# Decoding attention with a gated feed-forward on one core: inputs packed in order of use, all products on TensorE

## The chip, the cores and the metric

The kernel runs on one core of a Trainium2 chip. The metric is device microseconds of one execution, as the median of several runs. A core has TensorE (PE; its weight loads are PEld), VectorE (DVE), ScalarE (ACT), GpSimd (POOL) and SyncE (SP, which here only issues transfers), an on-chip memory of 128 partitions (SBUF), accumulators for TensorE (PSUM), and 16 DMA engines that move data between the chip's memory and SBUF. Everything is float32.

## The reference

One token goes through an attention block over a cached context of 8192 positions, then through a gated feed-forward block, each behind a layer norm and with a residual:

```python
B, Sq, D = 1, 1, 640
H, Sk, Dh = 32, 8192, 192        # k_cache, v_cache: (1, 32, 8192, 192)
...
q = (layernorm(x) @ wq) split into 32 heads of 192
scores = einsum("bhqd,bhkd->bhqk", q, k_cache) * (Dh ** -0.5)
o = einsum("bhqk,bhkd->bhqd", softmax(scores), v_cache)
h = x + o @ wo                    # wq (640, 6144), wo (6144, 640)
...
gate, up = layernorm(h) @ W_gate, layernorm(h) @ W_up      # (640, 1536)
h2 = h + (relu(gate) * up) @ W_down                        # (1536, 640)
```

K and V are 201 MB each, and all weights together 43 MB. Every byte is read once and used for one product, so the work is a stream of 446 MB.

## The kernel before

The work goes head by head, in the program order of one Python loop; a tile framework puts in the waits.

**Transfers.** SP issues all loads in program order. `load_kv` (L77 to L84) brings K or V of one head as one transfer of 128 partitions with 49,152 bytes each into one of three buffers `kv_t`; a load is issued when the tile that had this buffer has been used up. `load_wo` (L86 to L92) brings the rows of `wo` for four heads (two at the end). `wq` comes first, in three transfers through the same buffers. The last loads are W_up, W_gate in two parts and W_down in six (L359 to L363). In all SP issues 89 loads of 128 partitions each: 32 of K, 36 for V (the last head's in five), 9 of `wo`, 3 of `wq`, and 9 for the feed-forward; each partition's piece is a packet on one of the 16 DMA engines, so each engine moves 8 packets per load.

**Scores.** In `head_step` (L181 to L194) DVE multiplies K with the query in four pieces (L188), POOL adds the upper half of each product to the lower (L189), and DVE sums what is left (L193).

**Softmax** (`softmax_steps`, L196 to L215): maximum over partitions through a TensorE transpose (L200), exponential on ACT (L206), the sum over partitions on TensorE (L208).

**Values.** In `values_of` (L234 to L256) TensorE takes 40 of the 64 positions of a partition, as 20 products of two positions with 384 columns (`pairs`, L226 to L231), ACT scales 12 (L240) and DVE 12 (L241), and POOL adds these up (L246). The last two heads' values go to TensorE entirely (`values_last`).

**After a head** `finish_steps` (L289 to L321) sums over partitions on TensorE (L299), transposes on DVE (L303) and multiplies with `wo` (L276, L319). At the end come the layer norm (L368 to L387), the two projections (L392) and the product with W_down (L409), which starts on each part of W_down as it lands, and one output transfer (L413).

A matmul in float32 shows as two records of PE, each with its weight load; four matmuls on the four groups of 32 columns of the array run side by side, and four such records are called a set below.

Of the kernel before, what the change touches and what calls it, by code (L numbers as in the profile page):

```python
# [1 line left out]

# [8 lines left out]
AX = mybir.AxisListType  # L11


@with_exitstack
def kernel(
    ctx: ExitStack,
    tc: tile.TileContext,
    x: bass.AP,
    kc: bass.AP,
    vc: bass.AP,  # L20
    wq: bass.AP,
    wo: bass.AP,
    w_gate: bass.AP,
    w_up: bass.AP,
    w_down: bass.AP,
    out: bass.AP,
):
# [48 lines left out]

    def load_kv(src, h, parts):  # L77
        t = kv.tile([P, 2 * TW], F32, name="kv_t")
        v = src[h].rearrange("(p r) d -> p (r d)", p=P)
        b = 0  # L80
        for n in parts:
            nc.sync.dma_start(t[:, b:b + n], v[:, b:b + n])  # L82
            b += n
        return t  # L84

    def load_wo(gi):  # L86
        hs = GROUPS[gi]
        j = len(hs) * DH // P
        t = wts.tile([P, j, D], F32, tag="wo_t", name="wo_t")
        r0 = hs[0] * DH  # L90
        nc.sync.dma_start(t, wo[r0:r0 + len(hs) * DH, :].rearrange("(p j) n -> p j n", p=P))
        return t  # L92

    ones = const.tile([P, P], F32, name="ones")
    nc.gpsimd.memset(ones, 1.0)
    eps = const.tile([P, 1], F32, name="eps")
    nc.gpsimd.memset(eps, EPS)
    ident = const.tile([P, P], F32, name="ident")
    from concourse.masks import make_identity
    make_identity(nc, ident)  # L100

    sel = const.tile([P, NQ, P], F32, name="sel")
    nc.gpsimd.memset(sel, 0.0)
    for g in range(NQ):
        nc.gpsimd.memset(sel[g * Q:g * Q + 1, g, :], 1.0)

    par = const.tile([P, 2, Q], F32, name="par")
    for i in range(2):
        nc.vector.reduce_sum(par[:, i, 0:1], ident.rearrange("p (g c) -> p g c", c=Q)[:, :, i], axis=AX.X)
        nc.vector.tensor_copy(par[:, i, 1:Q], par[:, i, 0:1].to_broadcast([P, Q - 1]))  # L110

    def rstd_of(dst, var, name):

        ve = const.tile([P, 1], F32, name=f"ve{name}")
        nc.vector.tensor_scalar_add(ve, var, EPS)
        sd = const.tile([P, 1], F32, name=f"sd{name}")
        nc.scalar.activation(sd, var, AF.Sqrt, bias=eps)
        y = const.tile([P, 1], F32, name=f"y{name}")
        nc.vector.reciprocal(y, sd)
        t = const.tile([P, 1], F32, name=f"t{name}")  # L120
        nc.vector.scalar_tensor_tensor(t, y, ve, y, op0=ALU.mult, op1=ALU.mult)
        nc.vector.tensor_scalar(t, t, -0.5, 1.5, op0=ALU.mult, op1=ALU.add)
        nc.vector.tensor_mul(dst, y, t)


    s1 = const.tile([P, 1], F32, name="s1")
    nc.vector.reduce_sum(s1, xT, axis=AX.X)  # L127
    pm = ps_s.tile([P, 512], F32, name="ps_small")
    nc.tensor.matmul(pm[:, 0:1], ones, s1, start=True, stop=True)
    mean = const.tile([P, 1], F32, name="mean")  # L130
    nc.vector.tensor_scalar_mul(mean, pm[:, 0:1], 1.0 / D)
    xc = const.tile([P, DJ], F32, name="xc")
    nc.vector.tensor_scalar(xc, xT, mean, None, op0=ALU.subtract)
    xsq = const.tile([P, DJ], F32, name="xsq")
    nc.vector.tensor_mul(xsq, xc, xc)
    s2 = const.tile([P, 1], F32, name="s2")
    nc.vector.reduce_sum(s2, xsq, axis=AX.X)
    pv = ps_s.tile([P, 512], F32, name="ps_small")
    nc.tensor.matmul(pv[:, 0:1], ones, s2, start=True, stop=True)
    var = const.tile([P, 1], F32, name="var")  # L140
    nc.vector.tensor_scalar_mul(var, pv[:, 0:1], 1.0 / D)
    rstd = const.tile([P, 1], F32, name="rstd")
    rstd_of(rstd, var, "x")
    xn = const.tile([P, DJ], F32, name="xn")
    nc.vector.tensor_scalar_mul(xn, xc, rstd)


    acc = ps_a.tile([P, DG], F32, name="acc")
    for g in range(NQ):
        nc.tensor.matmul(acc[g * Q:(g + 1) * Q, :], ones[0:1, 0:Q], xrow[:, g * DG:(g + 1) * DG],  # L150
                         start=True, stop=False)


    qps = [ps_q.tile([P, QB], F32, tag="q", name=f"qp{b}") for b in range(2)]
    qps.append(ps_x.tile([P, QB], F32, tag="x", name="qp2"))
    for j in range(DJ):
        for b in range(NQB):
            for g in range(NQ):
                c0 = g * HPQ * DH + b * QB
                nc.tensor.matmul(qps[b][g * Q:(g + 1) * Q, :], xn[:, j:j + 1].to_broadcast([P, Q]),  # L160
                                 wq_ts[j][:, c0:c0 + QB], start=(j == 0), stop=(j == DJ - 1))
    q4 = const.tile([P, HPQ * DH], F32, name="q4")
    for b in range(NQB):
        nc.scalar.mul(q4[:, b * QB:(b + 1) * QB], qps[b], SCALE)  # L164

    pair_of = {}

    def query(h):

        g, i = divmod(h, HPQ)  # L170
        if i % 2 == 0:
            q = ps_q.tile([P, QB], F32, tag="q", name="q")
            nc.tensor.matmul(q[:, 0:2 * DH], sel[:, g, :], q4[:, i * DH:(i + 2) * DH], start=True, stop=True)  # L173
            pair_of[h // 2] = q
        return pair_of[h // 2][:, (i % 2) * DH:(i % 2 + 1) * DH]

    HD = DH // 2

    keep = tc.keep_in_program_order

    def head_step(q, kt, *works):  # L181


        sc = small.tile([P, NS], F32, name="sc")
        k3 = kt.rearrange("p (r d) -> p r d", d=DH)
        parts = [(i0, k3[:, i0:i0 + SUB, :]) for i0 in range(0, NS, SUB)]
        for i0, ks in parts:
            keep(nc.vector.tensor_mul(ks, ks, q[:, None, :].to_broadcast([P, SUB, DH])))  # L188
            nc.gpsimd.tensor_add(ks[:, :, 0:HD], ks[:, :, 0:HD], ks[:, :, HD:DH])  # L189
            for w in works:  # L190
                next(w, None)
        for i0, i1 in ((0, NS // 2), (NS // 2, NS - SUB), (NS - SUB, NS)):
            keep(nc.vector.reduce_sum(sc[:, i0:i1], k3[:, i0:i1, 0:HD], axis=AX.X))  # L193
        return sc  # L194

    def softmax_steps(sc, res):  # L196
# [15 lines left out]
        keep(nc.vector.reciprocal(rl, pl[:, 0:1]))  # L212
        nc.scalar.mul(pn, p, rl)  # L213
        res += [pn]
        yield  # L215

# [123 lines left out]
    for _ in done:  # L342
        pass
# [97 lines left out]
```

## Time and profile before

| what | before |
|---|---|
| median of 3 runs | 1044.37 us (1044.22 to 1044.38) |
| profiled execution, from first to last instruction | 1042.8 us |
| DVE, POOL busy | 779.6 us (75%), 776.5 us (74%) |
| PE, ACT busy | 311.4 us (30%), 161.8 us (16%) |
| loads: share of the 16 DMA engines' span | 99.3% |
| moved | 446.28 MB, 428 GB/s |

The profile has no time of its own for the profiled execution beside its span of 1042.8 us; the median of the runs is 1.6 us above this span. That is what lies around the span: the runs count from before the first recorded instruction to after the last. Sums below are made against the span, and 1.6 us is added at the end. Shares are of the span; "idle before" in a group of instructions is the time that its engine stood still just ahead of it, with the releaser behind the arrow.

### The profile page before, as it was taken

What the parts mean: (1) busy time and instruction counts of PE and PEld (TensorE: products, weight loads), DVE (VectorE), ACT (ScalarE), POOL (GpSimd) and SP (SyncE); (2) the same over time, 40 slices, a digit from 0 to 9 for tenths busy, and PEclk for the clock granted to TensorE, in tenths of its full rate; (3) what the DMA queues carried; (4) which work ended last, traced back from release to release, by engine and by line L of the source; (5) the groups of instructions that cost most, each with busy time, mean ns of one, the idle gap of its engine ahead of it and who ended that gap; (6) DMA issues with size and microseconds to landing.
All of it is one profiled execution on the core that took longest, in us unless ns stands there. A gap on an engine that the chain in (4) does not pass through costs nothing.

```text
span 1042.8 us, 5875 instructions
## 1 busy us (share of the span) xinstructions
PE 311.4 (30%) x2056; PEld 91.5 (9%) x2056; DVE 779.6 (75%) x445; ACT 161.8 (16%) x471; POOL 776.5 (74%) x321
## 2 busy tenths in 40 slices
PE   1603232222234212232322222242222323230376
PEld 0100000000000000000000000000000000010122
DVE  1087988688888888688986888788886889878641
ACT  0101111011111101111110111111111111110110
POOL 0057888788887888688897888868886888888730
PEclk9955655665656556566666656565565665565577
DMA  9999999999999999999999999999999999999997
GB/s 392 446 430 432 425 441 426 437 427 436 432 434 430 428 438 424 439 425 440 432 432 430 434 432 430 433 432 434 430 423 441 436 432 430 432 436 424 433 423 307
DMA packets 12998, 446.28 MB, mean 428 GB/s; under 512 B 1573, under 2 KB 1577, under 8 KB 3114
## 3 DMA queue, kind: packets, MB, share of 16 engines
q1 hardware_dynamic: 12824, 445.92, 99.3%
q8 instruction: 16, 0.26, 0.1%
q14 instruction: 12, 0.10, 0.0%
q10 hardware_dynamic: 146, 0.01, 0.0%
HBM read 445.91 MB, written 0.00 MB: 428 GB/s over the span
## 4 chain that ended last, share of the span: by engine, by line
DMA 77%; DVE 14%; PE 5%; POOL 3%; issue 1%; ACT 0%; SPq 0%; ACTq 0%; POOLq 0%; DVEq 0%
DMA kv_t<-in_A_k_cache_dram 70%; DVE kv_t L188 12%; DMA ffn_b<-in_B_W_down_dram 3%; PE ps_small L299 2%; DMA kv_t<-in_A_v_cache_dram 2%; DMA xrow<-in_A_x_dram 2%; POOL kv_t L246 2%; PE ps_small L200 1%; POOL kv_t L189 1%; DVE sc L193 1%; PE qp L160 1%; DVE kv_t L241 1%; DVE mp L198 0%; PE pd L409 0%; SPq L82 0%
## 5 line engine op out<-in xcount | busy, mean ns | idle before, releaser
L188 DVE TENSOR_TENSOR kv_t<-kv_t,q 128x3072 f32<-128x3072 f32 x128 | 427.4, 3342 | 182.8 <-DMA kv_t<-in_A_k_cache_dram 182.4
L189 POOL TENSOR_TENSOR kv_t<-kv_t 128x1536 f32<-128x1536 f32 x128 | 438.2, 3448 | 96.1 <-DVE kv_t L188 85.1
L246 POOL TENSOR_TENSOR kv_t<-kv_t 128x1152 f32<-128x1152 f32 (+1 forms) x180 | 337.2, 1874 | 125.7 <-DVE kv_t L241 80.7
L193 DVE TENSOR_REDUCE sc<-kv_t 128x16 f32<-128x1536 f32 (+1 forms) x96 | 213.2, 2273 | 0.7 <-POOL kv_t L189 0.7
L230 PE MATMUL po<-kv_t,pn 128*2 128x384 f32 x1328 | 162.0, 653 | 104.1 <-DMA kv_t<-in_A_v_cache_dram 104.1
L200 PE MATMUL ps_small<-ident,mp 128*128 128x128 f32 x32 | 14.2, 444 | 449.0 <-DVE mp L198 449.0
L240 ACT ACTIVATE kv_t<-kv_t,pn 128x192 f32<-128x192 f32 x360 | 127.8, 441 | 101.9 <-DMA kv_t<-in_A_v_cache_dram 98.4
L241 DVE TENSOR_TENSOR kv_t<-kv_t,pn 128x2304 f32<-128x2304 f32 x30 | 103.3, 3444 | 0.0
L206 ACT ACTIVATE p<-sc,m 128x64 f32<-128x64 f32 x32 | 11.1, 348 | 583.7 <-DVE m L203 583.7
L230 PEld LDWEIGHTS po<-kv_t,pn 128*2 128x2 f32 x1328 | 38.1, 103 | 219.1 <-issue 219.1
L200 PEld LDWEIGHTS ps_small<-ident,mp 128*128 128x128 f32 x32 | 5.8, 180 | 471.7 <-issue 426.9
L276 PE MATMUL acc<-wo_t,oT 128*3 128x480 f32 x112 | 32.8, 898 | 18.0 <-DVE oT L303 18.0
L173 PE MATMUL q<-q,sel 128*128 128x384 f32 x32 | 20.7, 747 | 56.9 <-DVE kv_t L188 56.9
L208 PE MATMUL ps_small<-rs,ones 128*128 128x1 f32 x64 | 18.6, 359 | 59.7 <-ACT p L206 59.7
L213 ACT ACTIVATE pn<-p,rl 128x64 f32<-128x64 f32 x32 | 11.1, 348 | 102.7 <-DVE rl L212 102.7
L299 PE MATMUL ps_small<-kv_t,ones 128*32 128x192 f32 (+1 forms) x64 | 24.8, 508 | 2.2 <-POOL kv_t L246 2.2
L208 PEld LDWEIGHTS ps_small<-rs,ones 128*128 128x128 f32 x64 | 15.8, 307 | 86.2 <-ACT p L206 74.5
L303 DVE STREAM_TRANSPOSE oT<-ps_small 32x192 f32<-32x192 f32 (+1 forms) x32 | 11.7, 364 | 10.2 <-PE ps_small L299 9.5
L160 PE MATMUL qp<-kv_t,xn 128*32 128x512 f32 x120 | 17.2, 737 | 5.5 <-DMA kv_t<-in_A_wq_dram 3.1
L242 DVE TENSOR_TENSOR kv_t<-po,par 128x384 f32<-128x384 f32 x30 | 16.3, 544 | 0.0
L268 DVE MEMSET acc<- 128x512 f32 x1 | 0.5, 485 | 20.9 <-ACT q L164 20.9
L127 DVE TENSOR_REDUCE s<-xT 128x1 f32<-128x5 f32 x1 | 0.2, 157 | 17.1 <-DMA xT<-in_A_x_dram 17.1
(82 smaller groups left out, 102.7 us busy)
## 6 DMA issues: line engine op xcount, KB each, us to landing
kv_t<-in_A_k_cache_dram SPq DMA_DIRECT2D x32, 6144.0 KB, 24.1
kv_t<-in_A_v_cache_dram SPq DMA_DIRECT2D x31, 6144.0 KB, 23.2
wo_t<-in_A_wo_dram SPq DMA_DIRECT2D x7, 1920.0 KB, 27.1
kv_t<-in_A_wq_dram SPq DMA_DIRECT2D x2, 6144.0 KB, 17.8
ffn_a<-in_B_W_up_dram SPq DMA_DIRECT2D x1, 3840.0 KB
kv_t<-in_A_wq_dram SPq DMA_DIRECT2D x1, 3072.0 KB, 40.0
kv_t<-in_A_v_cache_dram SPq DMA_DIRECT2D x1, 3072.0 KB, 17.2
kv_t<-in_A_v_cache_dram SPq DMA_DIRECT2D x4, 768.0 KB, 20.8
```

What stands on the lines that cost most here:

```text
L160: nc.tensor.matmul(qps[b][g * Q:(g + 1) * Q, :], xn[:, j:j + 1].to_broadcast([P, Q]), wq_ts[j][:, c0:c0 + QB], start=(j == 0), stop=(j == ...
L188: keep(nc.vector.tensor_mul(ks, ks, q[:, None, :].to_broadcast([P, SUB, DH])))
L189: nc.gpsimd.tensor_add(ks[:, :, 0:HD], ks[:, :, 0:HD], ks[:, :, HD:DH])
L193: keep(nc.vector.reduce_sum(sc[:, i0:i1], k3[:, i0:i1, 0:HD], axis=AX.X))
L200: keep(nc.tensor.transpose(pt[:, 0:P], mp.to_broadcast([P, P]), ident))
L208: nc.tensor.matmul(pl[:, 0:1], ones, rs, start=True, stop=True)
L230: nc.tensor.matmul(po[g * Q:g * Q + 2, :], pn[:, 2 * i:2 * i + 2], vt[:, 2 * i * DH:(2 * i + 2) * DH], start=(i < NQ), stop=(i >= n - NQ))
L240: nc.scalar.activation(v3[:, r, :], v3[:, r, :], AF.Copy, scale=pn[:, r:r + 1])
L241: keep(nc.vector.tensor_mul(v3[:, RV:NS, :], v3[:, RV:NS, :], pn[:, RV:NS, None].to_broadcast([P, RN, DH])))
L246: nc.gpsimd.tensor_add(v3[:, r:r + n, :], v3[:, r:r + n, :], v3[:, s:s + n, :])
L276: nc.tensor.matmul(acc3[g * Q:g * Q + 3, 0:W3], oT[:, t:t + 3, 0], w3[:, g * W3:(g + 1) * W3], start=(gi == 0 and t == 0), stop=(gi == LAS ...
L299: nc.tensor.matmul(pt[q0:q0 + Q, 0:W], par[:, k, :] if n > 1 else ones[:, 0:Q], ob[:, k * DH + u * W:k * DH + (u + 1) * W], start=(k == 0) ...
```

## The change

The kernel is written anew, without the tile framework.

- **Packing.** On the host (`pack`) the inputs are laid out in the order of use, 128 partitions wide. A turn of three heads is five rows: four of 65,280 bytes a partition and one of 56,832. K comes transposed (the 192 elements of a position across partitions), the columns of `wq` for a head and the rows of `wo` for a head lie beside it. A first row of 57,088 bytes holds head 0's K, the first query weights and x; four tail rows hold the last heads, and W_up, W_gate and W_down follow, W_down in four pieces. That makes 61 loads of 128 partitions.
- **Buffers.** Three slots X, Y, Z of 65,280 bytes a partition. Row 1 goes to X, 2 to Z, 3 to Y, 4 to X, 5 to Y. A slot is loaded again when semaphores say that all of it has been used.
- **Products.** TensorE computes queries (from a DVE product, L392 to L394), scores (24 matmuls of 512 columns a head, `pe_k`), values (32 of 384 columns a head, `pe_v`) and the head's output (`pe_o`). DVE transposes scores, takes maxima and adds the `wo` product; ACT copies and takes the exponential; POOL only fills constants.
- **Loops.** Each engine has its own program; ten turns run as a hardware loop on PE, DVE, ACT and SP.

```diff
-        for i0, ks in parts:
-            keep(nc.vector.tensor_mul(ks, ks, q[:, None, :].to_broadcast([P, SUB, DH])))
-            nc.gpsimd.tensor_add(ks[:, :, 0:HD], ks[:, :, 0:HD], ks[:, :, HD:DH])
...
-            kt = load_kv(kf, h + 1, [2 * TW])
-            vt = load_kv(vf, h, [2 * TW])
...
+DOWN = ((0, 6 * D), (6 * D, 10 * D), (10 * D, 11 * D + D // 2), (11 * D + D // 2, 12 * D))
...
+        rows[0][i] = cat(kw[a], qw(b), va[:, :8 * PW])
+        rows[1][i] = cat(va[:, 8 * PW:], ow(a - 1), kw[b][:, :12 * 512])
+        rows[2][i] = cat(kw[b][:, 12 * 512:], qw(c), vb[:, :24 * PW])
+        rows[3][i] = cat(vb[:, 24 * PW:], ow(b - 1), kw[c])
+        rows[4][i] = cat(qw(c + 1), vv, ow(c - 1))
...
+    def pe_k(blk, before=(None, None)):
+        for half in range(2):
+            if before[half] is not None:
+                wait(te, before[half], 16)
+            for part in range(3):
+                for g in range(4):
+                    m = te.matmul(sc[Q(g), half * 512:half * 512 + 512], qs[:, 32 * part:32 * part + 32],
+                                  blk(half, part * 4 + g), start=(part == 0), stop=(part == 2))
+            op(m, inc=p2d)
...
+            m = te.matmul(po[32 * g:32 * g + 2, 0:PW], p[:, 2 * i:2 * i + 2], blk(i), start=(i < 4), stop=(i >= 28))
...
+        with te.Fori(0, NTURN):
+            wait(te, land[1], 16)
+            pe_unit(ka, (None, None), va, (land[2], None), free[1], inc_at=(7, free[1]))
+            pe_unit(kb, (None, land[3]), vb, (None, land[4]), free[3], inc_at=(23, free[3]))
+            pe_unit2()
...
+    def dve_unit(wo_t, w_next, relay=None, q_wait=None):
+        dve_scores()
+        if relay is not None:
+            wait(ve, ds, cnt.n).then_inc(relay, 1)
...
+            dve_unit(woa, wqb)
+            dve_unit(wob, wqc, relay=free[2])
+            wait_row5 = (land[5], 16)
+            dve_unit(woc, wqa, relay=free[4], q_wait=wait_row5)
+            settle()
+            ve.sem_inc(free[5], 1)
...
+        def turn(i):
+            load(Y[:, 0:W_3], r3[i], land[3])
+            wait(sp, free[1], 2, 2)
+            wait(sp, land[1], 16, 16)
+            load(X[:, 0:W_4], r4[i], land[4])
+            wait(sp, free[2], 1, 1)
+            wait(sp, land[2], 16, 16)
+            wait(sp, free[3], 2, 2)
+            wait(sp, land[3], 16, 16)
+            load(Y[:, 0:W_5], r5[i], land[5])
+            wait(sp, free[4], 1, 1)
+            wait(sp, land[4], 16, 16)
+
+        with sp.Fori(0, NTURN - 1) as i:
+            turn(i)
+            load(X[:, 0:W_1], r1[i + 1], land[1])
+            load(Z[:, 0:W_2], r2[i + 1], land[2])
+            wait(sp, free[5], 1, 1)
+            wait(sp, land[5], 16, 16)
...
+        for n, (a, b) in enumerate(DOWN):
+            load(X[:, W_UP + a:W_UP + b], dram["row_down"][:, a:b], tl[f"d{n}"])
```

SP's loads in the steady stage before, one head and a half (names in brackets are the framework's semaphores of the engines and of earlier loads):

```order
L82 DMA kv_t<-in_A_k_cache_dram 128x12288 [waits DVE_49,DMAHW2_49,PE_49,Activation_49]
L82 DMA kv_t<-in_A_v_cache_dram 128x12288 [waits DMAHW6_49,DMAHW3_49,DVE_49]
L91 DMA wo_t<-in_A_wo_dram 128x3840
L82 DMA kv_t<-in_A_k_cache_dram 128x12288 [waits DVE_49,DMAHW4_49,PE_49,Activation_49]
L82 DMA kv_t<-in_A_v_cache_dram 128x12288 [waits DMAHW5_49,DVE_49]
```

SP's loop of one turn now (`land` counts a row that has landed, `free` says that a slot is used up):

```order
L544 DMA slot_y<-row 128x16320
L544 DMA slot_x<-row 128x16320 [waits free1,land1]
L544 ISA [waits free2,land2,free3,land3]
L544 DMA slot_y<-row 128x14208
L544 ISA [waits free4,land4]
L544 DMA slot_x<-row 128x16320
L544 DMA slot_z<-row 128x16320
L567 REGISTER_ALU [waits free5,land5]
L567 COMPARE_AND_BRANCH
```

Six transfers of K and V and three quarters of one of `wo` have become five; each load still stands behind waits for its slot. The load of the next turn's row 1 into X waits for `free4`, which DVE gives after it has transposed the scores of the turn's third head.

PE in the steady stage before, one head:

```order
L299 MATMUL ps_small<-kv_t,ones 32x192 [waits Pool_49]
L208 MATMUL ps_small<-rs,ones 128x1 [waits Activation_49]
L230 MATMUL po_217<-kv_t,pn 2x384 [waits DMAHW7_49,Activation_49]
L230 MATMUL po_217<-kv_t,pn 2x384 x19
L200 MATMUL ps_small<-ident,mp 128x128 [waits DVE_49,PE_49]
```

PE now, from the landing of row 4 to the landing of row 5 and the values behind it:

```order
L194 MATMUL po<-slot_x,p 2x384 [waits land4]
L194 MATMUL po<-slot_x,p 2x384 x7
L210 MATMUL od<-mrl,ob 128x1 [waits a2p]
L210 MATMUL od<-mrl,ob 128x1
L213 MATMUL od<-mrl,ob 64x1 x4
L218 MATMUL pl<-rs,ones 128x1 [waits a2p]
L187 MATMUL sc<-slot_x,qs 32x512 x24
L194 MATMUL po<-slot_y,p 2x384 [waits land5]
L194 MATMUL po<-slot_y,p 2x384 x23
```

The scores of a head, which were DVE's and POOL's, stand on PE as 24 matmuls, and the values of a head are 32 matmuls in place of 20.

## Rows read from the trace of the kernel before

**Rows 1.** The page's head and its busy time of each engine: share of span, instructions.

```profile
span 1042.8 us, 5875 instructions
PE 311.4 (30%) x2056; PEld 91.5 (9%) x2056; DVE 779.6 (75%) x445; ACT 161.8 (16%) x471; POOL 776.5 (74%) x321
```

**Rows 2.** The page's DMA lines and queues: packets, MB, share of 16 engines' span.

```profile
DMA  9999999999999999999999999999999999999997
GB/s 392 446 430 432 425 441 426 437 427 436 432 434 430 428 438 424 439 425 440 432 432 430 434 432 430 433 432 434 430 423 441 436 432 430 432 436 424 433 423 307
...
q1 hardware_dynamic: 12824, 445.92, 99.3%
q8 instruction: 16, 0.26, 0.1%
q14 instruction: 12, 0.10, 0.0%
```

**Rows 3.** The chain of waits in order of time: start us, us, what.

```profile
230.50 24.12 DMA kv_t<-in_A_k_cache_dram
254.65 3.35 DVE kv_t L188
...
283.71 3.35 DVE kv_t L188
...
317.37 3.35 DVE kv_t L188
...
1036.17 3.47 PE pd L409 x48
```

**Rows 4.** The costliest groups of the page that the change removes or widens.

```profile
L188 DVE TENSOR_TENSOR kv_t<-kv_t,q 128x3072 f32<-128x3072 f32 x128 | 427.4, 3342 | 182.8 <-DMA kv_t<-in_A_k_cache_dram 182.4
L189 POOL TENSOR_TENSOR kv_t<-kv_t 128x1536 f32<-128x1536 f32 x128 | 438.2, 3448 | 96.1 <-DVE kv_t L188 85.1
L230 PE MATMUL po<-kv_t,pn 128*2 128x384 f32 x1328 | 162.0, 653 | 104.1 <-DMA kv_t<-in_A_v_cache_dram 104.1
```

**Rows 5.** Timeline of PE at the last head's values: start us, us, engine, instruction.

```profile
1006.69 7.04 PE L230 MATMUL po<-kv_t,pn 128*2 128x384 f32 x64
...
1007.70 0.17 PEld L230 LDWEIGHTS po<-kv_t,pn 128*2 128x2 f32 x4 [0.47 <-issue]
1008.34 0.17 PEld L230 LDWEIGHTS po<-kv_t,pn 128*2 128x2 f32 x4 [0.47 <-issue]
...
1011.28 0.11 PEld L230 LDWEIGHTS po<-kv_t,pn 128*2 128x2 f32 x4 [0.21 <-issue]
1011.61 0.11 PEld L230 LDWEIGHTS po<-kv_t,pn 128*2 128x2 f32 x4 [0.21 <-issue]
```

**Rows 6.** Windows at the end: us, each engine's busy us, PE's granted clock, DMA share, GB/s.

```profile
1006.70:1010.40 3.70, 3.70 (x32) 1.08 (x32) 0.00 (x0) 0.34 (x2) 0.00 (x0) 0.54 1.11 470
1010.40:1013.70 3.30, 3.30 (x44) 0.88 (x35) 0.00 (x0) 0.00 (x0) 0.00 (x0) 1.00 0.95 410
1019.90:1024.00 4.10, 4.07 (x28) 1.38 (x32) 0.28 (x2) 0.00 (x0) 0.00 (x0) 0.50 0.98 417
1024.00:1030.70 6.70, 5.00 (x56) 1.34 (x48) 0.00 (x0) 0.58 (x1) 0.00 (x0) 1.00 1.01 421
```

**Rows 7.** Groups by form: small work whose like is on the change's path.

```profile
L261 ACT COPY obl<-po 128x384 f32<-128x384 f32 x2 | 1.0, 480 | 17.6 <-PE po L230 17.6
L404 DVE STREAM_TRANSPOSE guT<-gu 128x384 f32<-128x384 f32 x1 | 0.8, 845 | 0.0
```

**Rows 8.** Timeline: a sum over partitions, SP's first loads and the end.

```profile
1018.30 0.56 PE L382 MATMUL ps_small<-hs,ones 128*128 128x1 f32 x2 [1.13 <-DVE hs L380]
0.75 1.33 SPq L74 DMA_DIRECT2D kv_t<-in_A_wq_dram  x3
1036.17 3.43 PE L409 MATMUL pd<-ffn_b,guT 128*32 128x160 f32 x48 [0.91 <-DMA ffn_b<-in_B_W_down_dram]
1039.67 0.38 DVE L412 SCALAR_TENSOR_TENSOR o<-pd,hr,h 128x160 f32<-128x160 f32 x1 [7.46 <-PE pd L409]
```

**Rows 9.** Windows around the first and the last byte that is loaded.

```profile
0.00:1.70 1.70, 0.00 (x0) 0.00 (x0) 0.76 (x2) 0.00 (x0) 1.14 (x9) 1.00 0.00 0
...
1037.00:1038.00 1.00, 1.00 (x20) 0.76 (x16) 0.00 (x0) 0.00 (x0) 0.00 (x0) 0.50 0.26 100
1038.00:1039.00 1.00, 1.00 (x21) 0.75 (x16) 0.00 (x0) 0.00 (x0) 0.00 (x0) 0.50 0.00 0
```

More of the change, by code (lines that the diff above doesn't have):

```diff
@@ L1 @@
-from contextlib import ExitStack
+import concourse.bacc as bacc
 import concourse.bass as bass
-import concourse.tile as tile
 from concourse import mybir
-from concourse._compat import with_exitstack
 F32 = mybir.dt.float32
@@ L416 @@
-_INS = ['A_x', 'A_k_cache', 'A_v_cache', 'A_wq', 'A_wo', 'B_W_gate', 'B_W_up', 'B_W_down']
-_OUTS = [((1, 1, 640), 'float32')]
-def kernel(**inputs):
-    import numpy as _np
-    import concourse.bacc as _bacc
-    import concourse.tile as _tile
-    from concourse import mybir as _mybir
-    from concourse.bass_utils import run_bass_kernel_spmd as _run
-    nc = _bacc.Bacc("TRN2", target_bir_lowering=False, num_devices=1)
-    arrays, args = {}, []
-    for name in _INS:
-        a = _np.ascontiguousarray(inputs[name])
-        arrays[f"in_{name}_dram"] = a
-        args.append(nc.dram_tensor(f"in_{name}_dram", a.shape, _mybir.dt.from_np(a.dtype), kind="ExternalInput").ap())
-    for i, (shape, dtype) in enumerate(_OUTS):
-        dt = _mybir.dt.from_np(_np.dtype(dtype))
-        args.append(nc.dram_tensor(f"out_{i}_dram", shape, dt, kind="ExternalOutput").ap())
-    with _tile.TileContext(nc) as tc:
-        kernel(tc, *args)
-    r = _run(nc, [arrays], core_ids=[0])
-    got = tuple(r.results[0][f"out_{i}_dram"] for i in range(len(_OUTS)))
-    return got[0]
+ET = mybir.EngineType
@@ new lines @@
+P, D, H, S, DH, F = 128, 640, 32, 8192, 192, 1536
+DJ, FJ = D // P, F // P
+NS = S // P
+KW = NS * DH
+QW = DJ * DH
+OW = 960
+PW = 2 * DH
+NPAIR = NS // 2
+NTURN = (H - 2) // 3
+SCALE = DH ** -0.5
+EPS = 1e-5
+DG, FG = D // 4, F // 4
+W_P = 14272
+W_1 = KW + QW + 8 * PW
+W_2 = 24 * PW + OW + 12 * 512
+W_3 = 12 * 512 + QW + 24 * PW
+W_4 = 8 * PW + OW + KW
+W_5 = QW + KW + OW
+W_T1 = KW + 8 * PW
+W_T2A = 24 * PW + OW
+W_T2B = 16 * PW
+W_T3 = 16 * PW + OW
+W_UP = DJ * F
+DOWN = ((0, 6 * D), (6 * D, 10 * D), (10 * D, 11 * D + D // 2), (11 * D + D // 2, 12 * D))
@@ new lines, in pack, with kt, qw, ow @@
+def pack(inputs):
+    import numpy as np
+    x = np.ascontiguousarray(inputs["A_x"]).reshape(P, DJ)
+    kc = np.ascontiguousarray(inputs["A_k_cache"])[0]
+    vc = np.ascontiguousarray(inputs["A_v_cache"])[0].reshape(H, P, KW)
+    wq = np.ascontiguousarray(inputs["A_wq"]).reshape(P, DJ, H, DH)
+    wo = np.ascontiguousarray(inputs["A_wo"]).reshape(H, DH, D)
+    def kt(h):
+        k = kc[h].reshape(4, 32, 32, 2, DH).transpose(4, 3, 0, 2, 1).reshape(DH, 2, 4, 2, 512)
+        a = k[:P]
+        b = k[P:].transpose(1, 0, 2, 3, 4).reshape(P, 4, 2, 512)
+        r = np.stack([a[:, 0], a[:, 1], b], 1)
+        return r.transpose(0, 3, 1, 2, 4).reshape(P, KW)
+    def qw(h):
+        return wq[:, :, h].reshape(P, QW)
+    def ow(h):
+        w = wo[h]
+        r = np.concatenate([w[P:, 0:D // 2], w[P:, D // 2:]], 0)
+        return np.concatenate([w[:P], r], 1)
+    cat = lambda *a: np.concatenate(a, 1)
+    kw = [kt(h) for h in range(H)]
+    out = {"row_p": cat(qw(0), kw[0], qw(1), x, np.zeros((P, W_P - 2 * QW - KW - DJ), np.float32))}
+    rows = [np.empty((NTURN, P, w), np.float32) for w in (W_1, W_2, W_3, W_4, W_5)]
+    for i in range(NTURN):
+        a, b, c = 3 * i + 1, 3 * i + 2, 3 * i + 3
+        va, vb, vv = vc[a - 1], vc[b - 1], vc[c - 1]
+        rows[0][i] = cat(kw[a], qw(b), va[:, :8 * PW])
[3 more added lines that the diff above has]
+        rows[4][i] = cat(qw(c + 1), vv, ow(c - 1))
+    for n, r in enumerate(rows):
+        out[f"row_{n + 1}"] = r
+    h = H - 1
+    out["row_t1"] = cat(kw[h], vc[h - 1][:, :8 * PW])
+    out["row_t2a"] = cat(vc[h - 1][:, 8 * PW:], ow(h - 1))
+    out["row_t2b"] = np.ascontiguousarray(vc[h][:, :16 * PW])
+    out["row_t3"] = cat(vc[h][:, 16 * PW:], ow(h))
+    out["row_up"] = np.ascontiguousarray(inputs["B_W_up"]).reshape(P, DJ * F)
+    out["row_gate"] = np.ascontiguousarray(inputs["B_W_gate"]).reshape(P, DJ * F)
+    out["row_down"] = np.ascontiguousarray(inputs["B_W_down"]).reshape(P, FJ * D)
+    return {k: np.ascontiguousarray(v) for k, v in out.items()}
@@ new lines @@
+def kernel(**inputs):
+    from concourse.bass_utils import run_bass_kernel_spmd
+    arrays = pack(inputs)
+    nc = bacc.Bacc("TRN2", target_bir_lowering=False, num_devices=1, dynamic_dma_scratch_size=2048)
+    build(nc, arrays)
+    nc.compile()
+    r = run_bass_kernel_spmd(nc, [arrays], core_ids=[0])
+    return r.results[0]["out"]
```

755 lines of the change are left out of this document (416 added, 339 removed).

## The prediction, made before the change was timed

> **What bounds the kernel now.** I read the page from the top: busy time, DMA lines, queues, then the chain of waits, then the end by timeline and windows. No engine is the bound: DVE and POOL are busy for three quarters of the span, PE for 30% [rows 1]. The DMA line shows a 9 in all slices but the last, and the load queue alone fills 99.3% of the 16 engines' span [rows 2]. The reader is to see that this is not one busy stretch among others: 0.993 x 1042.8 = 1035.5 us is transfer, and only 7 us are anything else. Of these, 1.7 us go by before the first byte, and 4.8 us behind the last one (no byte moves after 1038.0, the span ends at 1042.8) [rows 9]. DVE's multiplies show 182 us of waiting for K [rows 4]; that wait is the stream's, not a gap in it.
>
> The stream's rate comes from the chain of waits. From one head's first multiply to the next are 29.06 us, and 33.66 us where a load of wo lies between [rows 3]. Per engine, the first is 16 packets of 49,152 bytes; the second has 8 packets of 15,360 bytes more. With a time a for each packet and b for each byte, 16a + 786,432b = 29.06 and 8a + 122,880b = 4.60, so b = 36.7 ps (27.2 GB/s an engine) and a = 0.011 us. The times are read to 0.01 us, which leaves a between 0.008 and 0.013. So a packet of 49 KB spends 0.6% of its time on being a packet. Larger packets can win little, and work taken off DVE and POOL nothing at all.
>
> **The change, part by part.**
>
> *Bytes.* 870,976 columns of 512 bytes make 445.94 MB; the queue moved 445.92 [rows 2]. Zero.
>
> *Packets.* 89 loads of 8 packets an engine are 712; 89 x (128 + 16 completions) plus 8 for the output is the queue's 12,824 [rows 2]. The 61 loads of the change make 488. 224 x 0.011 = **-2.4 us**, between -1.8 and -2.9. No work hides this, since every engine's queue is full throughout.
>
> *Engine work, off the path.* The multiplies and adds of DVE and POOL for the scores (427 and 438 us [rows 4]) go, with those for the values. TensorE gets them. A set of four 384-column records takes 0.64 us at the granted clock of 0.54 and 0.33 us at 1.00, which are the levels of 1.2 and 2.4 GHz [rows 5, 6]. A head's 32 value matmuls are 16 sets, 10.2 us at 1.2 GHz; its 24 score matmuls are 12 sets of 512 columns, 12 x 0.64 x 512/384 = 10.2 us. A turn's rows take 8 x (65,280 x 36.7 ps + 0.011) = 19.3 us each for rows 1 to 4 and 16.8 us for row 5, together 94 us or 31.3 us a head. With some 6 us for small products and hand-overs, TensorE needs 26.5 us even if it never leaves 1.2 GHz. Cost zero while this holds; the cover is 5 us a head.
>
> *Waits for slots.* SP stands behind free slots, and everything later stands behind SP, so each load is costed against the transfer that must cover it. I count all at 1.2 GHz. Row 4 waits for 16 value matmuls behind row 2's landing: 5.1 us, covered by row 3's 19.3. Row 5 waits for half of the scores and 24 value matmuls behind row 3's landing: 5.1 + 7.7 us and a start of 1 us, covered by row 4's 19.3. Row 3 waits for all of row 5, but rows 1 and 2 (38.6 us) are ahead of it. The close one is row 1 of the next turn, which goes to X when DVE has transposed the third head's scores; it must be covered by row 5's 16.8 us. After row 4 lands: 8 value matmuls 2.6 us [rows 5]; ACT's copy 0.48 [rows 7]; six small products, each between a third of and the full 0.56 of one with 128 weight columns [rows 8], say 2.4; one of 0.56; the scores 10.2; the second transpose, 0.845 x 512/384 = 1.1 [rows 7]; from SP's issue at 0.75 to the first byte at 1.7 [rows 8, 9], 1.0; hand-overs of 0.07 (PE's end at 1039.60 to DVE's start at 1039.67 [rows 8]), six of them 0.4. That is 18.7 us if PE stays at 1.2 GHz throughout and 13.6 us with the scores at 2.4 GHz. It passes if no more than 6.4 us of the scores run cold. Two bursts of before rose to 2.4 GHz 3.7 and 4.1 us after they began [rows 6], and here the burst begins 6 us ahead of the scores. I take 2.4 GHz for most of them: zero, with about 2 us in hand.
>
> *Engine code.* 4112 records of PE [rows 1] came in the 16 packets, 0.26 MB, of one instruction queue, 64 bytes a record; both instruction queues hold 0.36 MB and 0.1% of the engines' time, about 1 us [rows 2]. The loop's body on PE has 3 x 67 matmuls of four records, 51 KB, the rest of its program 63 KB. If the body is fetched once, code falls to about a third: -0.6 us. No row shows a branch back, so the other end is a fetch in each of ten turns: 0.58 MB, +0.7 us. I take 0. [...]
>
> *Start.* SP issues its first load behind one branch, as before: 0, at most +0.5.
>
> *End.* Before, six of the twelve steps of the W_down product were still to be done when their parts landed at 1036.17: 12 sets in 3.43 us at 0.50, 0.29 each, to 1039.60, which is 1.6 us behind the last byte [rows 8, 9]. Now four steps land 1.6 us ahead of the last byte (8 x (3,840 + 1,280 bytes) and their packets), then one and a half, then a half. At 1.2 GHz these are 14 set times, 4.0 us, 2.4 us behind the last byte; at 2.4 GHz 0.5. So between -1.1 and +0.8. The clock was 1.00 until 1030.7 [rows 6] and 0.50 over the last steps [rows 9]. I take -0.3. The work ahead of it (last values, layer norm, two projections of 6.4 us each at most) has 27.6 us of feed-forward loads over it.
>
> **Sum.** -2.4 + 0 + 0 - 0.3 = -2.7 us: a span of 1040.1, and with the 1.6 us that lie around it **1041.7 us**, 0.26% less. The bounds of its terms, not all met at once, give 1039.4 to 1043.2. The runs of before lie within 0.2 us; what a measurement can tell from no change is 0.2%, 2.1 us, so faster means under 1042.3.
>
> **Rivals.**
>
> *Row 1 comes late (slower).* A wait takes the place of none: SP issues row 1 after the engines have emptied their queues, once a turn. For it: the sum above is 18.7 against 16.8 us with a cold clock, and PE stands still ahead of row 4, since its work on row 3 ends about 13 us after that landed and row 4 takes 19.3. Against it: the rises within 4.1 us [rows 6]. It decides from 6.4 us of cold scores. Fully cold, 1.9 us in each of ten turns: 1061 us. Half of that is 1051. Chance 0.13.
>
> *Code comes back in each turn and the end runs cold (no change).* PE's fetch then queues behind a data packet of 65,280 x 36.7 ps = 2.4 us and takes about 1 us itself; PE ends a turn's work some 13 us after row 5 lands and row 1 lands 19.3 us after it, so the stall is covered. What remains is +0.7 for the traffic and +0.8 at the end against -2.4: 1043.5 us. [...] For it: the clock of 0.50 over the last steps. Chance 0.18.
>
> *The same code packets fall on few engines (slower).* The loads are shared evenly, so an engine with more code finishes last. Forty packets of 1 us on four engines would be 10 us: 1051 us. Against it: today's 16 such packets leave the DMA line full to the last slice [rows 2]. Chance 0.05.
>
> *TensorE doesn't keep up, or the rows move more slowly.* 26.5 against 31.3 us speaks against the first; the second would need a packet of 65 KB to cost more per byte than one of 49 KB, where 15 KB and 49 KB follow one line [rows 3]. 1% in rate would be 1052. Chance 0.04.
>
> **How the numbers follow.** Forecast 0.60: 0.52 of it ends under 1042.3, 0.08 within 0.2%. Code and a cold end: 0.18, within 0.2%. Row 1 late 0.13: 0.02 of it so little that it stays within 0.2%, 0.11 slower. Code on few engines 0.05 and slow rows or PE 0.04: slower. So faster 0.52, same 0.28, slower 0.20. The range goes from 1039.2 to 1049: it leaves out little below and, above, the worse half of the slow cases.
>
> **What would show it.** The load queue at 99% of the span again with some 8,800 packets; the chain of waits nearly all DMA; POOL empty, DVE under a quarter, PE above 40%; SP's waits ending ahead of the engines' queues, and the DMA line without a dent. PE's end 0.5 to 2.4 us behind the last byte. It is wrong if the DMA line dips once in each 94 us, if the instruction queues hold more than 0.6 MB, or if the last W_down steps stand behind the layer norm and not behind the loads.

## The result: slower by 0.24%, and the profile after

The changed kernel takes 1047.05 us (median of nine runs, 1044.64 to 1048.95), the kernel before 1044.47 (nine runs, 1044.22 to 1044.72): a ratio of 1.0024, interval 1.0014 to 1.0033. That is 2.6 us slower where 2.7 us faster was forecast. The runs of the change also scatter by 4.3 us, those of before by 0.5. Of the runs below, two of the four executions of `e8_row1_latest`, its profiled one among them, are left out of its ratio as slow.

The page of the changed kernel: head, busy times, GB/s in 40 slices of 26 us, queues, section 4 (chain), costliest groups.

```profile
span 1045.8 us, 10227 instructions
PE 562.2 (54%) x4480; PEld 181.9 (17%) x4480; DVE 189.7 (18%) x474; ACT 40.8 (4%) x136; POOL 1.2 (0%) x11
...
DMA  9999999999999999999999999999999999999998
GB/s 399 438 438 424 419 439 439 436 412 429 434 408 432 439 440 432 437 429 416 439 432 432 413 437 414 433 434 439 424 413 439 437 421 436 422 437 431 414 424 344
...
q1 hardware_dynamic: 8788, 445.94, 99.1%
q8 instruction: 7, 0.11, 0.0%
q14 instruction: 1, 0.01, 0.0%
...
PE 0%; DVE 0%; issue 0%
...
L187 PE MATMUL sc<-slot_x,qs 128*32 128x512 f32 x1008 | 152.3, 767 | 95.1 <-DMA slot_x<-row 85.0
L194 PE MATMUL po<-slot_y,p 128*2 128x384 f32 x1152 | 122.3, 579 | 46.5 <-DMA slot_y<-row 43.7
```

The engines look as intended: POOL is empty, DVE fell from 75% to 18% of the span, PE rose from 30% to 54% [rows 1], and PE's idle time ahead of scores and values is nearly all put down to loads, as DVE's was before [rows 4]. The load queue moved the same bytes in 8,788 packets, not 12,824 [rows 2]. Yet it fills 99.1% of a longer span. The digits of the DMA line, all 9 but the last, hide the loss; the GB/s line shows it. Before, no slice between the first and the last fell under 423 [rows 2]; here seven of them lie at 408 to 416, and a turn of 94 us is 3.6 slices. The chain of waits, which named the loads before [rows 3], is of no use: this kernel's waits are instructions of their own, and the chain breaks off after the last 2 us (0% for each engine). So the bound has to be read from landings.

PE's timeline of the changed kernel, from row 4's landing (first line) to row 5's (last line) in the first turn, and row 5's landings in turns 2 and 10 (start us, us, instruction, in brackets the idle time before it and what ended it):

```profile
98.71 2.74 PE L194 MATMUL po<-slot_x,p 128*2 128x384 f32 x16 [9.57 <-DMA slot_x<-row]
102.22 0.98 PE L210 MATMUL od<-mrl,ob 128*128 128x1 f32 x4 [0.77 <-PEq L134]
103.13 0.60 PE L213 MATMUL od<-mrl,ob 128*64 128x1 f32 x8
103.66 0.58 PE L218 MATMUL pl<-rs,ones 128*128 128x1 f32 x2
104.17 7.02 PE L187 MATMUL sc<-slot_x,qs 128*32 128x512 f32 x48
115.52 2.10 PE L194 MATMUL po<-slot_y,p 128*2 128x384 f32 x12 [4.33 <-DMA slot_y<-row]
...
209.40 5.75 PE L194 MATMUL po<-slot_y,p 128*2 128x384 f32 x48 [3.48 <-DMA slot_y<-row]
...
968.31 5.43 PE L194 MATMUL po<-slot_y,p 128*2 128x384 f32 x48 [4.05 <-DMA slot_y<-row]
```

SP's issues in the same places: row 5, then rows 1 and 2 of the next turn; and row 1 again a turn later.

```profile
88.55 0.33 SPq L544 DMA_DIRECT2D slot_y<-row  x1
112.37 0.33 SPq L544 DMA_DIRECT2D slot_x<-row  x1
112.80 0.37 SPq L544 DMA_DIRECT2D slot_z<-row  x1
...
207.09 0.33 SPq L544 DMA_DIRECT2D slot_x<-row  x1
```

Windows of the changed kernel (us, busy us of PE, PEld, DVE, ACT, POOL, PE's granted clock, DMA share, GB/s): ahead of row 4's landing, behind it, the scores.

```profile
88.00:98.60 10.60, 1.14 (x11) 0.63 (x7) 0.29 (x1) 0.24 (x1) 0.00 (x0) 0.78 0.99 427
98.60:104.10 5.50, 4.62 (x30) 2.29 (x30) 0.28 (x2) 0.87 (x3) 0.00 (x0) 0.50 0.95 413
104.10:111.20 7.10, 7.09 (x49) 1.69 (x49) 2.25 (x5) 0.00 (x0) 0.00 (x0) 0.76 1.05 451
```

PE stands still for 9.57 us ahead of row 4, works at a granted clock of 0.50 behind it, and comes back to 1.00 within the scores (0.76 on the mean). The prediction calls these two levels 1.2 and 2.4 GHz; the traces show the granted share alone. SP gives row 1 out at 112.37, and with the 1.0 us from issue to first byte [rows 8, 9] its bytes start at 113.4, 2.2 us before row 5 has landed at 115.52. In the second turn it is 208.1 against 209.40, 1.3 us. By the prediction that is in time. But from 115.52 to 968.31 are nine turns of 94.75 us, where the prediction's rate and price of a packet make 93.9 (it rounds this to 94).

### The profile page after: what moved, and what is told of

Its sections match the earlier page's. It is cut to its first block, busy times and chain, and to the rows that moved or that the text cites. A ratio compares the mean times of both kernels' runs of the same rounds, so it can differ in the third digit from the quotient of the medians.

```text
span 1045.8 us, 10227 instructions
## 1 busy us (share of the span) xinstructions
PE 562.2 (54%) x4480; PEld 181.9 (17%) x4480; DVE 189.7 (18%) x474; ACT 40.8 (4%) x136; POOL 1.2 (0%) x11
## 3 DMA queue, kind: packets, MB, share of 16 engines
q1 hardware_dynamic: 8788, 445.94, 99.1%
## 5 line engine op out<-in xcount | busy, mean ns | idle before, releaser
L187 PE MATMUL sc<-slot_x,qs 128*32 128x512 f32 x1008 | 152.3, 767 | 95.1 <-DMA slot_x<-row 85.0
L194 PE MATMUL po<-slot_y,p 128*2 128x384 f32 x1152 | 122.3, 579 | 46.5 <-DMA slot_y<-row 43.7
L194 PE MATMUL po<-slot_z,p 128*2 128x384 f32 x560 | 69.9, 650 | 107.9 <-DMA slot_z<-row 103.3
L400 DVE STREAM_TRANSPOSE st<-sc 128x512 f32<-128x512 f32 x64 | 45.9, 717 | 338.3 <-PE sc L187 338.3
L187 PE MATMUL sc<-slot_y,qs 128*32 128x512 f32 x288 | 55.7, 937 | 75.6 <-DMA slot_y<-row 75.1
L194 PE MATMUL po<-slot_x,p 128*2 128x384 f32 x336 | 43.5, 652 | 94.6 <-DMA slot_x<-row 94.6
L187 PEld LDWEIGHTS sc<-slot_x,qs 128*32 128x32 f32 x1008 | 36.0, 136 | 193.3 <-issue 107.4
L194 PEld LDWEIGHTS po<-slot_y,p 128*2 128x2 f32 x1152 | 30.5, 96 | 138.0 <-issue 84.0
L194 PEld LDWEIGHTS po<-slot_z,p 128*2 128x2 f32 x560 | 14.7, 100 | 153.1 <-DMA slot_z<-row 110.5
L394 DVE SCALAR_TENSOR_TENSOR prod<-slot_y,xn,prod 128x192 f32<-128x192 f32 x88 | 36.9, 419 | 3.1
L187 PE MATMUL sc<-slot_z,qs 128*32 128x512 f32 x240 | 27.8, 596 | 0.0
L394 DVE SCALAR_TENSOR_TENSOR prod<-slot_x,xn,prod 128x192 f32<-128x192 f32 x40 | 16.8, 419 | 1.4
```

Of the source, the lines that this page charges most:

```text
L187: m = te.matmul(sc[Q(g), half * 512:half * 512 + 512], qs[:, 32 * part:32 * part + 32], blk(half, part * 4 + g), start=(part == 0), stop=( ...
L194: m = te.matmul(po[32 * g:32 * g + 2, 0:PW], p[:, 2 * i:2 * i + 2], blk(i), start=(i < 4), stop=(i >= 28))
L394: dv(STT(prod, w3[:, j, :], xn[:, j:j + 1], prod, op0=ALU.mult, op1=ALU.add), w="self", inc=d2p if j == DJ - 1 else None)
L400: dv(ve.transpose(st[:, s], sc[:, s]), w=pd())
```

## The experiments

Theory A: row 1 goes out too late although its first byte comes ahead of row 5's end; some queues have run dry by then. Rival B: rows of 65 KB a partition are themselves slow, as packets or because two are out together. Rival C: the loop's branch stops something once a turn.

**Row 1 in two loads** (`e1_row1_in_two`). The first 16 KB a partition of row 1 lie over columns of X that the `wo` product of the second head reads last, so they may be loaded ahead of the third head's scores.

```diff
+            wait(ve, ds, cnt.n).then_inc(free6, 1)
             wait_row5 = (land[5], 16)
...
-            wait(sp, free[4], 1, 1)
+            wait(sp, free6, 1, 1)
             wait(sp, land[4], 16, 16)
+            part()
+            wait(sp, free[4], 1, 1)
...
-            turn(i)
-            load(X[:, 0:W_1], r1[i + 1], land[1])
+            turn(i, lambda: load(X[:, 0:SP1], r1[i + 1, :, 0:SP1], land[1]))
+            load(X[:, SP1:W_1], r1[i + 1, :, SP1:W_1], land[1])
```

> Theory A (row 1 of the next turn is issued when the first engines have already run dry, and the restart costs idle time and slow packets, some 7 us over ten turns): the first 16 KB a partition of row 1 now go out some 7 us earlier and cover 4.7 us, so the loss goes and only 80 more packets an engine at 0.011 us come on top: 1047.0 - 7 + 0.9 = about 1041 us, with a spread under 1 us. Theory B (packets of 65 KB, or two loads issued together, are slow in themselves) and theory C (the jump back of the loops costs the time): no gain, 1047 to 1048 us.

Measured: 1038.68 us (1038.53 to 1039.34), ratio 0.9946 (0.9932 to 0.9960), where A expected about 1041. SP's two issues of row 1 and PE's landing of row 5 in the first turn, then PE's scores and the landing in the tenth:

```profile
105.86 7.41 SPq L547 DMA_DIRECT2D slot_x<-row  x2
115.32 2.21 PE L196 MATMUL po<-slot_y,p 128*2 128x384 f32 x16 [3.47 <-DMA slot_y<-row]
...
949.72 8.24 PE L189 MATMUL sc<-slot_x,qs 128*32 128x512 f32 x48
961.06 4.05 PE L196 MATMUL po<-slot_y,p 128*2 128x384 f32 x48 [3.09 <-DMA slot_y<-row]
```

A turn takes 93.97 us. The first part of row 1 goes out at 105.86, 9.5 us ahead of row 5's landing. The loss is gone with nothing done to PE's clock (the scores take 8.24 us here), and although the 11 more loads add packets (10,372). A holds; C, which this leaves as it was, falls.

**Row 1 later** (`e2_row1_later`, `e8_row1_latest`). Transposes into a buffer that nobody reads stand ahead of DVE's release of X, three of them, then six.

```diff
+        for _ in range(slow):
+            dv(ve.transpose(st2, sc[:, 0:512]), w="self")
...
-            dve_unit(woc, wqa, relay=free[4], q_wait=wait_row5)
+            dve_unit(woc, wqa, relay=free[4], q_wait=wait_row5, slow=3)
```

> DVE does three more transposes before it frees X, so row 1 is issued some 2.4 us later in each turn. Theory A: every engine now stands still in each turn, 1.5 to 2.4 us times ten more: 1062 to 1071 us. Theories B and C: no change beyond 1 us, 1047 us.

> Six more transposes in place of three ahead of the release of X: row 1 goes out another 2.3 us later in each turn. Theory A: all engines are dry by then, so the whole delay counts, ten times 2.3 us on 1056.5: 1077 to 1082 us. If only the first engines were dry in the kernel with three, less: 1066 to 1075 us. Theories B and C: no change on 1056.5 us.

Measured: 1056.50 us (1054.48 to 1058.21), ratio 1.0116 (1.0101 to 1.0132), for the three; 1067.56 and 1081.94 us for the six, ratio 1.0289 (1.0226 to 1.0352), beside 1089.82 and 1089.94 in the executions that are left out. Both are slower, as A has it and B and C do not, but not by A's sizes: 1056.50 lies under its 1062 to 1071, and the two times with six lie one in each of its ranges, so they do not tell whether all engines are dry. Of `e2_row1_later`, GB/s and PE's landings of row 5 in turns 1 and 10, then SP's issues of row 1 in turns 1 and 2:

```profile
GB/s 396 436 436 444 388 436 436 395 436 436 431 400 436 436 436 394 436 436 400 431 436 451 384 431 436 439 421 433 433 407 433 436 420 415 436 436 395 421 436 346
...
115.50 0.82 PE L195 MATMUL po<-slot_y,p 128*2 128x384 f32 x4 [4.22 <-DMA slot_y<-row]
...
975.91 6.83 PE L195 MATMUL po<-slot_y,p 128*2 128x384 f32 x48 [4.34 <-DMA slot_y<-row]
...
114.70 0.33 SPq L547 DMA_DIRECT2D slot_x<-row  x1
...
210.43 0.33 SPq L547 DMA_DIRECT2D slot_x<-row  x1
```

The same of `e8_row1_latest`, landings and issues, in its execution of 1089.82 us:

```profile
115.41 0.83 PE L195 MATMUL po<-slot_y,p 128*2 128x384 f32 x8 [3.06 <-DMA slot_y<-row]
...
1006.67 5.75 PE L195 MATMUL po<-slot_y,p 128*2 128x384 f32 x48 [3.26 <-DMA slot_y<-row]
...
118.03 0.33 SPq L547 DMA_DIRECT2D slot_x<-row  x1
...
217.16 0.33 SPq L547 DMA_DIRECT2D slot_x<-row  x1
```

In `e2_row1_later` the dents are those of the change, only deeper: seven slices lie at 384 to 400, the first six of them three or four apart. A turn takes 95.60 and 99.03 us in these two traces.

**PE kept at work ahead of row 4** (`e3_pe_warm`). Forty matmuls into an accumulator that is overwritten before it is read stand ahead of PE's wait for row 4; no load, buffer or row is touched.

```diff
         if vwait[1] is not None:
+            pe_warm(WARM)
             wait(te, vwait[1], 16)
...
+    WARM = 10
```

> Forty more matmuls of 512 columns fill PE's pause ahead of row 4 (they write an accumulator that is overwritten before it is read), so the clock should be at 2.4 GHz when row 4 lands: values 1.3 in place of 2.7 us, scores 5.1 in place of 7.0. Theory A: row 1 is issued some 3 us earlier and most of the loss goes: 1040 to 1043 us. Theories B and C: no change, 1047 us.

Measured: 1038.26 us (1037.63 to 1038.38), ratio 0.9940 (0.9926 to 0.9953). PE's timeline of this kernel, as above:

```profile
96.81 1.47 PE L249 MATMUL pl<-ident,ones 128*32 128x512 f32 x12
98.66 1.47 PE L194 MATMUL po<-slot_x,p 128*2 128x384 f32 x16 [0.38 <-DMA slot_x<-row]
100.90 0.58 PE L210 MATMUL od<-mrl,ob 128*128 128x1 f32 x4 [0.77 <-PEq L134]
101.41 0.41 PE L213 MATMUL od<-mrl,ob 128*64 128x1 f32 x8
101.74 0.38 PE L218 MATMUL pl<-rs,ones 128*128 128x1 f32 x2
102.06 5.36 PE L187 MATMUL sc<-slot_x,qs 128*32 128x512 f32 x48
...
115.34 1.46 PE L194 MATMUL po<-slot_y,p 128*2 128x384 f32 x8 [7.93 <-DMA slot_y<-row]
...
960.79 6.29 PE L194 MATMUL po<-slot_y,p 128*2 128x384 f32 x48 [8.03 <-DMA slot_y<-row]
```

Its GB/s, its windows at the places shown above, SP's issues of row 1, and its load queue:

```profile
GB/s 403 441 441 422 427 436 441 434 423 436 435 443 418 441 437 435 423 436 434 441 433 431 427 441 436 420 437 441 436 419 441 436 426 442 428 436 438 422 425 350
...
88.00:98.60 10.60, 10.28 (x95) 3.12 (x87) 0.29 (x1) 0.24 (x1) 0.00 (x0) 1.00 0.99 423
98.60:102.00 3.40, 2.57 (x30) 1.42 (x30) 0.13 (x1) 0.87 (x3) 0.00 (x0) 1.00 0.93 401
...
108.58 0.33 SPq L547 DMA_DIRECT2D slot_x<-row  x1
...
202.77 0.33 SPq L547 DMA_DIRECT2D slot_x<-row  x1
...
q1 hardware_dynamic: 8788, 445.94, 99.5%
```

PE stays at a clock of 1.00 through the scores (1.00 from 102.0 to 107.5 us as well), the 16 value records take 1.47 us in place of 2.74 and the scores 5.36 in place of 7.02, and SP has row 1 out 3.8 us sooner, at 108.58. Between its ends no slice lies under 418. A turn is 93.94 us, as the prediction's rate makes it. Packets of 65 KB, two loads out together and the branch are all still there, so B and C fall. A had expected 1040 to 1043 us. No version of the study is faster; this one is 0.6% under the kernel before.

**The price of a packet.** `e4_rows_in_halves` is `e1_row1_in_two` with rows 2 to 5 in two halves each, 320 more packets an engine; `e7_before_halves` does the like in the kernel before. There 63 loads are split (the last head's V came in five already), which makes 504 more packets an engine, not the 512 of its expectation:

```diff
+    def halves(t, w, src, s):
+        h = w // 2
+        load(t[:, 0:h], src[:, 0:h], s)
+        load(t[:, h:w], src[:, h:w], s)
...
-        load(Z[:, 0:W_2], r2[0], land[2])
+        halves(Z, W_2, r2[0], land[2])
```

```diff
-            kt = load_kv(kf, h + 1, [2 * TW])
-            vt = load_kv(vf, h, [2 * TW])
+            kt = load_kv(kf, h + 1, [TW, TW])
+            vt = load_kv(vf, h, [TW, TW])
```

> The kernel with row 1 in two loads, with rows 2 to 5 in two halves each as well: 320 more packets an engine. If a packet costs 0.011 us, +3.5 us over the kernel with row 1 in two (2.6 to 4.2): about 1044.5 us. If large packets cost or gain nothing, the same time as that kernel; if 65 KB packets are slow in themselves (theory B), faster than it.

> The kernel before with K and V of each head in two loads of 24,576 bytes a partition: 512 more packets an engine. At the 0.011 us a packet of the prediction +5.6 us, 1050.0 us; at the 0.0056 us that rows 2 to 5 in halves gave +2.9 us, 1047.3 us. Rival (transfers aren't the bound before the change, DVE and POOL are): no change, 1044.4 us.

Measured: 1040.47 us (1040.37 to 1041.29), +1.79 over `e1_row1_in_two` where 2.6 to 4.2 were expected, 0.0056 us a packet; and 1048.98 (1048.77 to 1049.40), ratio 1.0043 (1.0029 to 1.0057), +4.57 over the kernel before beside it, 0.0091 us a packet, between the two expectations. The halves are slower, not faster, which speaks against B once more.

**The end.** `e5_one_output` and `e6_six_pieces` are `e3_pe_warm` with one edit each at the end: one output transfer from SP in place of two from ACT and SP, and W_down in six pieces, as large as before, in place of four.

```diff
-        load(out[0, 0, 0:D // 2].rearrange("(g n) -> g n", g=2), o4[31:33, :], out_s)
+        load(out[0].rearrange("o (g n) -> (o g) n", g=4), o4[0:P:32, :], out_s)
...
-DOWN = ((0, 6 * D), (6 * D, 10 * D), (10 * D, 11 * D + D // 2), (11 * D + D // 2, 12 * D))
+DOWN = tuple((a * D, b * D) for a, b in ((0, 3), (3, 6), (6, 9), (9, 10), (10, 11), (11, 12)))
```

> The kernel with the clock kept up (1038.3 us), with one output transfer of four partitions from SP, as before, in place of one of two partitions each from SP and ACT. From PE's last product to the end were 3.2 us before and 1.9 after the change. Theory: the smaller transfers on two queues save this 1.3 us; then 1039.2 to 1039.6 us. Rival: it is the framework's close of the program that has gone; then no change, 1038.1 to 1038.5 us.

> The kernel with the clock kept up (1038.3 us), with W_down in six pieces as before (3, 3, 3, 1, 1, 1 of the twelve steps). Theory of the prediction: the pieces decide how much of the product stands behind the last byte; one whole step instead of a half at 0.16 us a set and 16 more packets: +0.3 us, +1 us if the clock falls: 1038.5 to 1039.3 us. Rival: the end is set elsewhere (layer norm or projections late): no change.

Measured: 1038.33 us (1038.12 to 1039.02) and 1038.26 (1037.85 to 1038.41), against 1038.26. Neither edit does anything that can be measured; both rivals had it so.

## Why the prediction was wrong

**Waits for slots: the step that failed.** The sum under this heading came out well. From row 4's landing to row 1's first byte it gave 18.7 us cold and 13.6 with the scores at the clock of 1.00; 98.71 to 113.4 is 14.7. Row 5's cover was put at 16.8; 98.71 to 115.52 is 16.81. What failed is the cover, and with it "zero, with about 2 us in hand". A landing is the end of the last of the 16 engines, and the prediction let the cover run from one landing to the next. The semaphore updates and packet records of the traces part the engines (the records don't name them, but row 5's packets are told by their 56,832 bytes). In the first turn the sixteen updates for row 4 came from 96.77 to 98.67, and the sixteen last packets of row 5 ended from 113.15 to 115.01. So the first engine had nothing left 14.5 us after row 4's landing, not 16.8; over nine turns 13.6 to 15.7. Row 1's first byte was due 12.2 to 15.7 us after that landing. The 2 us in hand were the time by which the engines lie apart.

For nine refills of each profiled execution: the first byte (issue + 1.0) against row 5's landing; how long an engine stood between its last packet of row 5 and its first of row 1, and how long that first packet took, both as means over the engines; the turn; and what a turn loses on `e3_pe_warm`'s 93.94 us.

| kernel | first byte against landing, us | engine empty, us | first packet, us | us a turn | lost, us a turn |
|---|---|---|---|---|---|
| `e3_pe_warm` | 5.7 to 5.9 ahead | 0 | 2.41 | 93.94 | 0 |
| the change | 1.3 to 4.6 ahead | 0.37 | 2.92 | 94.75 | 0.8 |
| `e2_row1_later` | 0.2 behind to 0.1 ahead | 1.28 | 3.04 | 95.60 | 1.7 |
| `e8_row1_latest`, the execution of 1089.82 us | 3.5 to 3.7 behind | 4.61 | 3.05 | 99.03 | 5.1 |

The empty time and what the first packets take over 2.41 us make 0.9, 1.9 and 5.3 us, close to the loss. Within the change the empty time follows the first engine: 0.1 us in the fourth and eighth turns, where the first byte was due 1.2 us or more ahead of that engine's end, and 1.0 and 0.8 in the third and sixth, where it was due 0.8 to 0.9 behind it. Why the first packets behind a refill take 0.5 to 0.6 us longer, no run shows. Ten turns of 0.8 us are 8 of the 8.8 us between the change and `e3_pe_warm`.

**The rival "Row 1 comes late"** had the right place and the wrong price. It was to decide from 6.4 us of cold scores. In the first turn the scores lost 7.02 - 5.36 = 1.7 us to the clock, which is about 3.3 us of cold running; by its rule nothing should have been lost. The clock evidence was read too kindly as well: the two rises within 4.1 us came behind other work, with PE idle for 0 and 1.07 us ahead of them, and here it had stood still for 9.57 us. A mean of 0.76 from 104.1 to 111.2 puts the rise near 107.5, 8.8 us behind the first value matmul. PE's pause was named and then not costed.

**Packets.** The count was right, 8,788 to 8,800. The price of 0.011 us was too high by the two direct tries, 0.0056 and 0.0091: 224 packets are then -1.3 to -2.0 us, not -2.4. The packets' own times are nearer to it. Two of 24,576 bytes in `e7_before_halves` take 1.833 us on the mean, one of 49,152 before takes 1.822; two of 32,640 in `e4_rows_in_halves` take 2.419, one of 65,280 in `e3_pe_warm` 2.412. That last figure also bears out the rate, 2.41 us by the prediction; its line through two sizes with two unknowns could not have failed by itself.

**Engine code.** The two instruction queues went from 28 packets of 0.36 MB to 8 of 0.12. PE's program of 114 KB came once, 0.11 MB in 7 packets, for ten turns of the loop: three packets started by 106.9 us, the other four from 992.9 us on, none between. So the other end, a fetch in each turn, falls: a taken branch did not bring the body in again here. A code packet of 16,384 bytes took 0.97 us on the mean (1.07 before), about the 1 us of the rival; that a fetch waits behind a data packet of 2.4 us was the author's estimate, and no run shows such a wait. By the prediction's own rate, 1 us for 0.36 MB, the term is about -0.7, not 0.

**End.** It went better than -0.3. The chain of the changed kernel's last 2 us (start us, us, what):

```profile
1041.88 0.04 issue
1041.92 1.61 PE q_ps L332 x40
1043.53 0.40 PE q_ps L339 x8
1043.93 0.02 issue
1043.96 0.38 DVE o L479
```

Forty records, ten sets, take 1.61 us, 0.16 a set where the kernel before took 0.29 at a clock of 0.50 [rows 8, 9]: the end ran at a clock of 1.00 (1041.90 to 1043.93 us), the good end of the term's range. Of `e3_pe_warm`, the windows around the last byte (the same columns as above):

```profile
1033.50:1034.00 0.50, 0.50 (x22) 0.37 (x13) 0.00 (x0) 0.00 (x0) 0.00 (x0) 1.00 0.07 26
1034.00:1035.00 1.00, 0.90 (x24) 0.57 (x16) 0.07 (x1) 0.00 (x0) 0.00 (x0) 1.00 0.00 0
```

PE's work ends there at 1034.91, 0.9 us behind the last byte, where it was 1.6 before: -0.7. The rest stood in no term. From PE's end to the span's end are 1.9 us in the change, before 3.2 (1039.60 to 1042.8). `e5_one_output` and `e6_six_pieces` show that neither the split output nor the pieces of W_down bring this; what does, was not isolated. The way the program closes is what is left, and that is argued only.

**The whole.** Without the late row the change is worth 1038.26 - 1044.47 = -6.2 us, more than the -2.7 forecast. By spans (1042.8 and 1036.8) it is 6.0: the last byte comes about 4 us sooner (before 1034.0, where it was before 1038.0 [rows 9]), and the work behind it is about 2 us shorter. The load queue's packets took 99.3% of the span before and 99.5% of it in `e3_pe_warm`, 1035.5 and 1031.6 us, so nearly all of the 4 is the packets' own time. The 224 fewer packets are 1.3 to 2.0 of it by the tries. Another 1.8 is that the 8,320 packets of 49,152 bytes took 1.8224 us on the mean before, where such packets take 1.8189 in `e1_row1_in_two`; why, no run shows. What lies around the span is 1.2 us now, not the 1.6 that the sum added. The late row takes 8.8 back, and +2.6 us is what is measured. That 1047.05 lies within the range given is owed to the rivals that are slower, for which it was kept wide, and to two misses of opposite sign. The prediction called itself wrong if the DMA line dips once in each 94 us; the digits don't show it, the GB/s line and the landings do.

**The scatter** of 4.3 us is 0.8 in both cures. In the fourth turn of the profiled run SP gave row 1 out 20.84 us behind row 5, where it took 23.82 in the first, so the lateness differs from turn to turn. The fourth turn's scores took 5.36 us at a clock of 1.00, as in `e3_pe_warm`, the first's 7.02 at 0.76 and the third's 8.03 at 0.66: the lateness goes with the clock. Over nine turns SP gave row 1 out 11.2 to 14.7 us behind row 4's landing, in the order of the scores' times, 5.36 to 8.03 us. That the runs differ by the same was not tried apart.

## What to carry to other kernels

In a stream that fills the DMA queues, a load must be issued so early that its first byte comes ahead of the first engine's end of the load before it, not of the landing, which is the last engine's; here the engines lay 0.9 to 2.7 us apart in the change, 5.9 us ahead of the landing were enough and 1.3 to 2.5 were not. Write the margin down for each load of a turn, and treat "just in time" as a loss. When the time from landing to release runs through TensorE, cost it with the clock that PE has after the pause before it (here 0.50 behind 9.57 us); a few matmuls that keep PE at work, or splitting the load that waits, may then be worth more than the packing itself (here 8.8 and 8.4 us, against the 6.2 of the change without the late row). Where the digits of the busy lines are full, compare landings a turn apart: nine turns showed 0.8 us in 94 that neither the busy line nor the chain did.

## What the runs showed that was not expected

- Refilling the queues 1.3 to 4.6 us ahead of a landing cost 0.8 us a turn on the mean, at the landing 1.7 us: a part is engines standing empty, and a part first packets that take 2.9 to 3.0 us in place of 2.4 (the table above).
- Filler matmuls on an engine that is idle nearly half the time made a kernel that waits for memory 8.8 us faster: PE's clock of 0.50 behind its pause was on the path of the load's release.
- A packet of about 32 KB in place of half of one of 65 KB cost only 0.0056 us by the runs' times: 430 GB/s in `e1_row1_in_two`, 429 in `e4_rows_in_halves` over the span.
